# One v piece transposed by DMA ahead of the second weights, other first and last steps, in a fused attention and gated-product kernel

## The chip, the cores and the metric

The kernel runs on one core of a Trainium2 chip. The time is the device time of one execution in microseconds (us); most executions of one kernel agree within 0.3%. The granted clock is the share of TensorE's full rate that the profile's clock records give.

Engines are named as in the profile: PE is TensorE, DVE VectorE, ACT ScalarE, POOL GpSimd, SP SyncE. In the traces each of them keeps the order that the program gives: in experiment e3 below, ScalarE stands 3.7 us at one instruction of the norms, and the evictions behind it wait. GpSimd issues the loads that cast float32 to bfloat16. SyncE issues stores and DMA transposes.

## The reference

For each of four batches with 5824 tokens of 256 channels:

```python
qn = q / (norm(q, axis=tokens) + 1e-6);  kn = k / (norm(k, axis=tokens) + 1e-6)
s  = kn.T @ qn / tau                      # 256 x 256, tau = 1
a  = softmax(s, -1)                       # divided by (sum + 1e-9)
x  = v @ a                                # 5824 x 256
```

and over all 23296 tokens `((x @ w1) * (x @ w2)) @ w3 @ w_out`, with w1 and w2 of 256 x 1024, w3 of 1024 x 1024, w_out of 1024 x 256.

## The kernel before

The kernel folds the softmax matrix into w1 and w2 (`Wf`, one pair per batch) and w3 into w_out (`W_sb`, once). What remains for each chunk of 512 tokens and each of 8 column tiles j are two products `a` and `b` with transposed v (four 512-column matmuls), their elementwise product `ab`, and output products `o` (four 256-column matmuls).

Until `W_sb` exists the output products of batch 0 are deferred, and afterwards two steps' worth are made for each step. While batch n runs, q and k of batch n+1 are loaded in six pieces each and their product G (the scores) is slipped between the other matmuls.

GpSimd's queue carries the loads, and two kinds of waits that keep them apart:

```python
def gate():                                   # not before TensorE has got this far
    if last_ab[0] is not None:
        nc.gpsimd.tensor_copy(gate_t, last_ab[0][:1, :1])

def hold(src):                                # not before this transpose has landed
    nc.gpsimd.tensor_copy(gate_t, src)
...
        if b == 0:
            ...
            at(7.0, 0.5, lambda: transpose_half_on_pe(0, 1, 0, True))   # v piece 1 on TensorE
            at(8.0, 0.5, lambda: transpose_half_on_pe(0, 1, 1, False))
            at(15.0, 0.0, transpose_w3)                                 # DMA, SP
            at(15.0, 0.0, lambda: transpose_piece(0, 2))                # DMA, SP
            for jt in range(FT):
                at(26.0 + 1.2 * jt, 0.87, lambda jt=jt: w_unit(jt))     # w3 @ w_out
            moves = [("v", 0, 3, 29.0), ("qk", 1, 0, 38.0), ("qk", 1, 1, 43.0), ("v", 0, 4, 50.0), ("qk", 1, 2, 58.0)]
            moves += [("qk", 1, 3, 63.0), ("v", 0, 5, 70.0), ("qk", 1, 4, 81.0), ("qk", 1, 5, 87.0)]
            moves += [("v", 1, 0, 96.0), ("v", 1, 1, 106.0), ("v", 1, 2, 116.0), ("qk", 2, 0, 126.0)]
            t0, t1 = 57.0, 115.5              # the scores of batch 1 are spread over this stretch
...
        for nm, m, pi, t in moves:
            if before is not None:
                at(t, 0.0, lambda w=before: hold(...))   # the v piece moved before, transposed
            at(t, 0.0, gate)
            if nm == "qk":
                at(t, 0.0, lambda m=m, pi=pi: load_qk(m, pi))
                before = None
            else:
                at(t, 0.0, lambda m=m, pi=pi: load_piece("v", m, pi))
                at(t + 4.0, 0.0, lambda m=m, pi=pi: transpose_piece(m, pi))
                before = (m, pi)
```

The numbers after `at(` are a model clock of TensorE's work, which the emitter uses to sort instructions. They are no waits. So a load stands in GpSimd's queue in this order, and is issued when everything ahead of it in that queue is done. The all-reduce of the norms (`tot`, at t1 + 1) stands in the same queue.

"v 5" is the last v piece of batch 0, "q/k 1_4" the fifth q and k pieces of batch 1.

## Time and profile before

| | before |
|---|---|
| time, median of 6 | 573.16 us (572.88 to 575.41) |
| span of the profiled run | 571.7 us |
| PE busy | 559.4 us, 98% |
| last k piece of batch 0 landed | 31.5 us |
| first product with v | 40.69 us |
| w3 landed; its product starts | 59.8 us; 67.07 us |
| w3T and v 2 transposed (hold ends) | 72.96 us |

The timeline shows start, duration, engine and line, instruction, and in brackets the idle time before it and its releaser.

```profile
105.42 0.60 POOL L430 COPY gate_t<-vT 1x1 bf16<-1x1 bf16 x1 [12.71 <-DMA vT<-v]
...
111.29 1.04 POOL L426 COPY gate_t<-abs 1x1 bf16<-1x1 bf16 x1 [2.29 <-DVE abs L453]
112.27 0.53 POOL L106 DMA_DIRECT2D v<-in_v_dram  x1
...
127.40 0.18 POOL L430 COPY gate_t<-vTt 1x1 bf16<-1x1 bf16 x1 [14.05 <-DMA vTt<-v]
...
128.65 0.54 POOL L109 DMA_DIRECT2D k<-in_k_dram  x1
```

The hold of 105.42 ended late, but at 111.29 GpSimd waits for TensorE's progress (`gate_t<-abs`): the queue has caught up. Then v 5 is loaded, and k 1_4 cannot be issued before v 5 is transposed, at 127.4. TensorE meets k 1_4 at 139.19 without a wait. How small that slack is, the page does not say, but the trace does: the load issued at 128.65 landed at 138.89, 0.3 us ahead of its first use. k 1_5 landed at 143.72 and was first used at 148.74, so it had 5.0 us.

### The profile page before, as it was taken

The page shows a single profiled execution, that of the slowest core. Times are in us where ns is not written, and L with a number is a line of the kernel's source. Part 1 is how long each engine was busy: PE and PEld are TensorE (multiplying, and loading weights), DVE is VectorE, ACT ScalarE, POOL GpSimd, SP SyncE. Part 2 cuts the span into 40 slices and gives each one's busy share as a digit, 9 for nine tenths or more (in the row PEclk, how much of TensorE's full clock was granted, in tenths as well). Part 3 has the DMA queues.
Part 4 walks back from the last instruction along what each step waited for, and adds up shares of the span by engine and source line. Part 5 has one row for each costly group of instructions (what it writes and reads, how often), then busy time and mean ns, then how long its engine had stood idle before and what let it go on. Part 6 is the DMA issues. An engine that isn't in the chain of part 4 may idle for free.

```text
span 571.7 us, 10102 instructions
## 1 busy us (share of the span) xinstructions
PE 559.4 (98%) x3750; PEld 354.5 (62%) x3750; DVE 377.4 (66%) x612; ACT 337.7 (59%) x624; POOL 83.3 (15%) x164
## 2 busy tenths in 40 slices
PE   7789999999999999999999999999999999999997
PEld 4655576776666666666666666666665666666665
DVE  1047744788977567887776667778876656565564
ACT  0046644777856567776766567767766554454453
POOL 5250020303030111121030012031120000000000
PEclk9999999999999999999999999999999999999999
DMA  8999959869685697495661595665640325221011
GB/s 163 211 187 208 184 104 240 170 149 242 140 183 118 123 204 150 94 192 121 145 144 72 99 215 123 140 136 126 175 110 38 85 73 148 63 63 75 38 72 58
DMA packets 74560, 76.93 MB, mean 135 GB/s; under 512 B 54160, under 2 KB 58256, under 8 KB 74512
## 3 DMA queue, kind: packets, MB, share of 16 engines
q0 software_dynamic: 15504, 39.46, 39.3%
q1 hardware_dynamic: 58784, 36.64, 22.2%
q8 instruction: 29, 0.48, 0.3%
q10 hardware_dynamic: 224, 0.20, 0.1%
q14 instruction: 19, 0.16, 0.1%
HBM read 78.91 MB, written 23.86 MB: 180 GB/s over the span
## 4 chain that ended last, share of the span: by engine, by line
PE 92%; DMA 5%; DVE 1%; ACT 1%; POOL 1%; issue 0%; ACTq 0%; POOLq 0%
PE o L479 28%; PE a L438 27%; PE b L438 27%; PE G L188 5%; DMA k<-in_k_dram 5%; PE fold L349 2%; PE w L596 1%; ACT as L444 0%; ACT kr L279 0%; POOL k L109 0%; POOL q L109 0%; DVE abs L453 0%; PE sqk L221 0%; DVE vT L136 0%; DVE abs L455 0%
## 5 line engine op out<-in xcount | busy, mean ns | idle before, releaser
L453 DVE TENSOR_TENSOR abs<-as,b 128x512 bf16<-128x512 bf16 x336 | 230.5, 687 | 141.4 <-ACT as L444 130.3
L444 ACT CAST as<-a 128x512 bf16<-128x512 f32 (+1 forms) x384 | 216.1, 563 | 176.9 <-DVE abs L453 90.2
L438 PEld LDWEIGHTS <-Wf 128*128 128x128 bf16 x1536 | 149.2, 98 | 102.0 <-issue 1.9
L479 PE MATMUL o<-W_sb,abs 128*128 128x256 bf16 x1376 | 209.6, 273 | 0.1
L438 PE MATMUL a<-vT,Wf 128*128 128x512 bf16 x704 | 209.4, 379 | 0.2
L438 PE MATMUL b<-vT,Wf 128*128 128x512 bf16 x704 | 209.3, 379 | 0.0
L479 PEld LDWEIGHTS <-abs 128*128 128x128 bf16 x1376 | 134.5, 98 | 81.6 <-DVE abs L455 0.3
L197 DVE TENSOR_TENSOR acc<-acc,sq 128x1024 f32<-128x1024 f32 x66 | 80.4, 1219 | 0.4 <-ACT sq L185 0.3
L188 PE MATMUL G<-k,q 128*128 128x256 bf16 x276 | 49.9, 273 | 0.0
L185 ACT ACTIVATE sq<-q 128x512 f32<-128x512 bf16 x66 | 41.8, 634 | 0.0
L185 ACT ACTIVATE sq<-k 128x512 f32<-128x512 bf16 x66 | 41.6, 630 | 0.0
L426 POOL COPY gate_t<-abs 1x1 bf16<-1x1 bf16 x39 | 13.9, 355 | 167.7 <-DVE abs L453 167.0
L500 DVE COPY osb<-o 128x512 f32<-128x512 f32 x44 | 30.1, 685 | 0.7 <-PE o L479 0.7
L430 POOL COPY gate_t<-vT 1x1 bf16<-1x1 bf16 x17 | 4.4, 258 | 169.3 <-DMA vT<-v 134.0
L188 PEld LDWEIGHTS <-q 128*128 128x128 bf16 x276 | 27.0, 98 | 3.1
L499 ACT COPY osb<-o 128x512 f32<-128x512 f32 x44 | 25.8, 586 | 3.8 <-PE o L479 1.8
L279 ACT ACTIVATE kr<-row 128x256 f32<-128x256 f32 x1 | 0.4, 385 | 31.6 <-PE row L267 31.6
L109 POOL DMA_DIRECT2D q<-in_q_dram x29 | 15.7, 541 | 13.2 <-DMA k<-in_k_dram 6.0
L349 PE MATMUL fold<-w,e 128*128 128x512 bf16 x64 | 17.0, 380 | 0.5 <-DVE vT L136 0.4
L356 ACT ACTIVATE Wf<-fold,rs 128x512 bf16<-128x512 f32 x16 | 10.9, 688 | 8.1 <-PE fold L349 6.4
L244 DVE TENSOR_TENSOR dk<-sqk,ident 128x256 f32<-128x256 f32 x1 | 0.4, 425 | 21.3 <-PE sqk L221 21.3
L109 POOL DMA_DIRECT2D k<-in_k_dram x25 | 13.8, 551 | 3.7 <-DMA k<-in_k_dram 1.9
(89 smaller groups left out, 240.4 us busy)
## 6 DMA issues: line engine op xcount, KB each, us to landing
out_dram<-osb SPq DMA_DIRECT2D x44, 512.0 KB, 3.1
k<-in_k_dram POOLq DMA_DIRECT2D x19, 512.0 KB, 8.5
v<-in_v_dram POOLq DMA_DIRECT2D x19, 512.0 KB, 5.2
q<-in_q_dram POOLq DMA_DIRECT2D x18, 512.0 KB, 6.6
w_wout<-in_moe_w_dram POOLq DMA_DIRECT2D x1, 2048.0 KB, 23.6
k<-in_k_dram POOLq DMA_DIRECT2D x4, 320.0 KB, 9.9
v<-in_v_dram POOLq DMA_DIRECT2D x4, 320.0 KB, 5.4
q<-in_q_dram POOLq DMA_DIRECT2D x4, 256.0 KB, 12.0
```

The lines of the kernel that those rows point to most:

```text
L109: nc.gpsimd.dma_start(out=pieces[nm, n, pi][:, lo:hi, :], in_=qk_main[nm, n][0][:, pi * PIECE + lo : pi * PIECE + hi, :])
L185: nc.scalar.activation(out=dst[:, :, part, :], in_=src[:, o : o + 2, :], func=AF.Square)
L188: nc.tensor.matmul(G[:, ct, :], lhsT=qt[:, i, ct * P : (ct + 1) * P], rhs=kt[:, i, :], start=(pr == 0 and part == 0 and ct == 0), stop=(pr ...
L197: nc.vector.tensor_add(accs[n], accs[n], sqs[0])
L349: nc.tensor.matmul(st["fold", i], lhsT=st["e"][:, c2, c1 * P : (c1 + 1) * P], rhs=w12[:, c2, w, h * 512 : (h + 1) * 512], start=(c2 == 0), ...
L426: nc.gpsimd.tensor_copy(gate_t, last_ab[0][:1, :1])
L438: nc.tensor.matmul(t[:, :n], lhsT=Wf[b][:, ct, w, j * P : (j + 1) * P], rhs=rhs_of(b, c, ct), start=(ct == 0), stop=(ct == CT - 1),)
L444: nc.scalar.copy(a_sb[:, :n], tiles[0][:, :n])
L453: nc.vector.tensor_mul(ab, a_sb, tiles[1])
L479: nc.tensor.matmul(tl[h][:, o, :], lhsT=lhsT, rhs=W_sb[:, j, :], start=(j == 0 and o == 0), stop=(j == FT - 1 and (small or o == 1)), skip ...
L499: nc.scalar.copy(o[:, 0:2, :], tl[0])
L500: nc.vector.tensor_copy(o[:, 2:4, :], tl[1])
```

## The change

Its intent: start earlier, spend less TensorE time on transposes, and make the changes of batch smoother. The diff, cut to its core:

```diff
-    busy(14)
-    load_piece("k", 0, 0, (half,))
-    load_piece("q", 0, 0, (half,))
+    busy(10)
+    for nm in "kq":                            # first halves: plain loads by SP, cast on chip
+        new_piece(nm, 0, 0)
+        raw[nm] = work.tile([P, half, C], F32, tag="o_sb", ...)
+        nc.sync.dma_start(out=raw[nm], in_=qk_main[nm, 0][0][:, :half, :])
+        load_part(nm, 0, 0, half, PIECE)
...
+            nc.tensor.matmul(                  # sums start from 1e-9: a float32 matmul, per batch
+                st["sum"][:, :CT], lhsT=tiny, rhs=ones_pp[:1, :CT], start=True, stop=False, ...)
...
-            fold_mm(0, 0) ... fold(5, "out")   # six folds and a transpose before the first product
+            quarter_mm(0, c1, 0) ... quarter_mm(0, c1, 1)       # a quarter before, the rest after it
...
-            + [(0.2, 15.5, sums)]
-            + [(0.43, 16.5 + 0.85 * i, lambda i=i: fold(i)) for i in range(8)]
+            + [(0.2, 16.5, sums)]
+            + [(0.43, 17.5 + 1.1 * i, lambda i=i: fold(i)) for i in range(8)]
...
-    nc.gpsimd.dma_start(out=wout_sb, ...)      # right behind the load of v 2
-    nc.gpsimd.dma_start(out=w3_bf, in_=w3r)
...
-            at(7.0, 0.5, lambda: transpose_half_on_pe(0, 1, 0, True))
-            at(8.0, 0.5, lambda: transpose_half_on_pe(0, 1, 1, False))
-            at(15.0, 0.0, transpose_w3)
-            at(15.0, 0.0, lambda: transpose_piece(0, 2))
+            at(0.0, 0.0, lambda: transpose_piece(0, 2))
+            at(0.0, 0.0, lambda: transpose_piece(0, 1))
+            at(0.0, 0.0, lambda: hold(vTs[0][0][:1, PIECE, 0, :1]))
+            at(0.0, 0.0, load_w3)
+            at(16.0, 0.0, transpose_w3)
-                at(26.0 + 1.2 * jt, 0.87, lambda jt=jt: w_unit(jt))
+                at(35.0 + 1.2 * jt, 0.87, lambda jt=jt: w_unit(jt))
-            moves = [("v", 0, 3, 29.0), ("qk", 1, 0, 38.0), ...                                  t0, t1 = 57.0, 115.5
+            moves = [("qk", 1, 0, 29.0), ("v", 0, 3, 30.0), ("qk", 1, 1, 43.0), ("qk", 1, 2, 47.0), ("v", 0, 4, 53.0)]
+            moves += [("qk", 1, 3, 62.0), ("qk", 1, 4, 66.0), ("v", 0, 5, 72.0), ("qk", 1, 5, 81.0)]
+            moves += [("v", 1, 0, 94.0), ("v", 1, 1, 104.0), ("v", 1, 2, 114.0), ("qk", 2, 0, 126.0)]
+            t0, t1 = 54.0, 113.0
-            t0, t1 = 16.0, 104.0               # later batches
+            t0, t1 = 16.0, 98.0
```

At the end, outputs run five behind in the last chunk, the 64 left-over rows are multiplied first, and the last two outputs swap. The cut leaves out that w1 and w2 are loaded in three ranges of columns instead of two, and smaller moves.

## The prediction

> **What bounds the kernel now.** I read the page's busy shares first, then the busy time in stretches, then the chain of work, then the DMA landings.
>
> The page gives TensorE 559.4 us of 571.7. The stretches say where the other 12 us are:
>
> ```profile
> core 0: us, PE busy (x) PEld busy (x) DVE busy (x) ACT busy (x) POOL busy (x), PEclk, DMA share, GB/s
> 0.00:31.50 31.50, 25.44 (x264) 19.20 (x264) 1.94 (x11) 1.28 (x1) 12.43 (x26) 1.00 1.00 188
> 31.50:37.00 5.50, 4.24 (x42) 3.12 (x42) 2.16 (x9) 2.57 (x8) 5.23 (x8) 1.00 1.13 166
> 37.00:40.70 3.70, 3.33 (x25) 1.66 (x26) 2.01 (x5) 2.32 (x4) 0.49 (x2) 1.00 1.18 192
> 40.70:67.10 26.40, 26.40 (x142) 12.73 (x141) 21.06 (x32) 17.58 (x30) 0.00 (x0) 1.00 1.05 199
> ...
> 170.00:183.00 13.00, 12.86 (x94) 7.92 (x93) 9.59 (x31) 8.41 (x20) 1.45 (x4) 1.00 0.66 160
> ...
> 303.00:315.00 12.00, 11.88 (x94) 8.31 (x92) 8.82 (x25) 7.81 (x18) 0.00 (x0) 1.00 0.11 44
> ...
> 436.00:449.00 13.00, 12.59 (x92) 7.90 (x90) 9.31 (x27) 7.92 (x18) 0.00 (x0) 1.00 0.11 42
> ...
> 561.80:572.00 10.20, 5.91 (x58) 4.92 (x56) 4.96 (x19) 3.41 (x10) 0.00 (x0) 0.95 0.22 77
> ```
>
> The reader sees that from 40.7 us on TensorE is full except at the three changes of batch and at the end; before 31.5 us the DMA share is 1.00. So there are two limits in series: the load of the first q and k, then TensorE's issue rate. Busy time flatters, since a matmul's record is longer than its turn: in the order of starts a 512-column matmul follows the last after 216 ns, a 256-column one after 109. Counting what starts exceed that by, the empty time is 0.90 us at 170 to 183, 0.58 at 303 to 315, 1.48 at 436 to 449, 0.54 after 560.
>
> The chain of work names the start:
>
> ```profile
> 4.52 11.89 DMA k<-in_k_dram
> 16.69 14.79 DMA k<-in_k_dram
> 31.53 0.84 PE sqk L221 x12
> ...
> 37.70 0.89 PE fold L349 x4
> 38.59 0.46 PE tr_I-511_512 L132 x8
> 39.05 0.02 issue
> 39.07 0.70 DVE vT L136
> 39.77 0.04 issue
> 39.82 1.04 PE fold L349 x4
> ```
>
> The last k piece lands at 31.5, the softmax of the first batch takes until 37.0, and then 3.7 us go by until the first product with v, with a stop at the evacuation of a transposed half of v.
>
> The weights' chain, from the DMA view and the timeline, matters for the rival:
>
> ```profile
> w_wout<-in_moe_w_dram POOLq DMA_DIRECT2D x1, 2048.0 KB, 23.6
> vT<-v SPq DMA_TRANSPOSE x22, 3.7
> w3T<-w_wout SPq DMA_TRANSPOSE x4, 4.4
> 67.07 1.04 PE L596 MATMUL w<-w_wout,w3T 128*128 128x256 bf16 x8
> ```
>
> w3, issued at 36.19, lands at 59.8; its transposes start at 59.85, and its product starts at 67.07, 3 us after the first transpose can have landed.
>
> **What the Trainium skill says.** "DMA: Bandwidth & Descriptors", section SWDGE vs HWDGE vs iDMA: a load that casts must come from GpSimd; loads issued by SP are plain, are fed to the same 16 engines on other queues, and each engine takes turns between them. So the new plain loads of the first halves add no bandwidth. The section "Latency and other measured facts" has a shorter time to the first byte for SP's path (about 0.6 against 1 us). The trace agrees in sign: an output issued by SP near 564.4 moves its first packet at 565.23 (some 0.85 us), the first load of GpSimd, issued at 1.22, at 2.60 (1.4 us). "TensorE: Matmul & The Clock Gate", The HAM clock gate, says that a fresh TensorE runs at half rate for about 3.4 us. The trace agrees: warm-up matmuls are 427 ns apart at first and 216 later. Taking four away at the start is harmless only while TensorE waits for loads anyway, which it does.
>
> **The change, part by part.**
>
> *First loads.* SP can issue at about 0.75 us (its start wait ends at 0.7), so data flow from about 1.65 instead of 2.60: 0.95 us. In addition the first 105 packets of before took 251 ns each, against 173 later, and moved only half the full rate until 4.5 us, a loss of about 0.85 us, part of which a second queue can fill. A plain 4096-byte packet takes 163 ns (outputs), a casting one with the same 4096 bytes read takes 173, so the plain loads are not dearer. The queue is then full until 28 us, so an earlier start carries through to 31.5. I book 1.2 us. The two casts (VectorE, ScalarE) lie where both engines idle. The last pieces are issued in the same eight-deep order, so they shift alike.
>
> *First folds.* Before, from 37.0 to the first product at 40.69: six folds and a transpose; afterwards two more folds (0.86 us) and three transposes (1.35). Changed: sums and a first quarter of 8 matmuls of 256 columns (0.87 us), one small operation less on the sums, evacuation of 256 columns (the kr activation of that size took 0.39, the scaling of s 0.42), so first product at about 38.6; afterwards the second quarter (0.87), four folds (1.73) and one transpose (0.45). TensorE time to the same point: 40.69 + 2.21 = 42.9 against 38.6 + 3.05 = 41.7. The two removed transposes (0.9 us) and the one moved into the wait for the exponentials (0.45) are in this; the second v piece is now transposed by the DMA. Gain 1.2, less 0.1 for a possible wait at the third product, whose factors VectorE delivers just then: 1.1 us.
>
> *Changes of batch.* The built order shows the sums earlier in all three, and in the last two the folds in pairs between 512-column products of chunk 10, where before three came at once; in the first they stand singly from chunk 11's start. A pair costs VectorE 0.69 + 0.75 us and ScalarE 0.56 + 0.69 in a step of 2.16 us on TensorE, and four PSUM buffers turn over once in a step, so these should not stop. At the chunk of 192 columns VectorE and ScalarE still have the outputs of chunk 10 to copy (0.69 and 0.59). I estimate 1.2 us of the 2.96 left: gain 1.75. Against it three extra float32 matmuls that start the sums: the float32 one already there (turned) has two passes 155 ns apart, so about 0.25 us each, 0.75 in all. Net gain 1.0 us.
>
> *End.* With a lag of five, ten output matmuls (1.1 us) cover the last evacuation, worth the 0.5 us that is empty now; but the first products of the last chunk come 0.33 us apart without outputs, while VectorE needs 0.4 to 0.5 each (0.29 + 0.21, partly overlapped), and the order of the two outputs moves the ACT-issued store 0.1 us later. I book zero.
>
> *Moved only.* w3's product has the same matmuls, later. Deferred outputs reach 43 pieces; before they were some 34. There is room for 54 (16 held in the q buffers, 38 in the pool).
>
> Sum: 1.2 + 1.1 + 1.0 = 3.3 us gained.
>
> **The rivals.**
>
> *The weights come too late.* w_out and w3 now wait for the transposes of v pieces 2 and 1. Before, piece 2 landed near 46.4; the smaller w1 and w2 loads (512-byte packets, 60 ns each, against 98 for 1024) cost about 0.5 us more, the earlier start gives 1.2 back: 45.7. Two transposes, 5.6 us: 51.3. Then 0.4 gate, 1.8 to the first packet, 3.4 for w_out, 10.2 for w3, 0.75 to land (their times of before): 67.9. First transpose of w3 usable 3.7 to 4.4 later: 71.6 to 72.3. The product's place in the order: 37.4 (38.6 less the load gain) + 37 products at 0.864 + 3.05 = 72.4. So the slack is zero to 0.8 us: a wait of 1 to 2 us is quite possible, and then TensorE stops, since nothing is ordered around it. I book 0.4 us as its mean. Further down, v piece 3 is usable at about 93 for a need near 94.6.
>
> *The first loads hide nothing*, if the slow first packets belong to the engines and not to the queue, or if the last small pieces of q are paced by their issue: then the load part is 0.5 or less, and the time about 570.9.
>
> *The batch changes don't improve*, because the float32 matmuls wait or the small chunk stays short of VectorE: then that part is minus 0.7, and the time 571.8.
>
> All three failing together with a 2 us wait would give no gain at all. None of these can come to 2% (11.5 us).
>
> **Range and chances.** 572.96 - 3.3 + 0.4 = 570.06, taken as 570.1. The best case (load 1.8, no wait, batch changes 1.7, end 0.4) gives 568; the poor ones 572. Range 568.4 to 572.1. Faster by over 2%: 0.01; within 2%: 0.97; slower: 0.02, for a starved stretch in batch 0 that I have not seen.
>
> **What would show it.** The last k piece should land near 30.3 and the first product with v start near 37.4. The first w matmul should start near 72.4 with no wait on w3T before it; a gap there makes the rival true. The empty time at the batch changes should fall from 2.96 to about 1.2 us without the new float32 matmuls. At the end, the gap before the last outputs should be gone and a few small ones appear at chunk 11. The prediction is wrong if the first products start no earlier than 38.5, or if TensorE stops for over 2 us between 72 and 130 us.

## More of the kernel before

The prediction reads the page. One row of it that the prediction leaves out matters later. It is from the costliest groups; the last columns are the engine's idle time just before the group, and what ended most of it:

```profile
L430 POOL COPY gate_t<-vT 1x1 bf16<-1x1 bf16 x17 | 4.4, 258 | 169.3 <-DMA vT<-v 134.0
```

GpSimd stands 169 us in the holds of this group. That alone costs nothing.

## The result, and the profile after

| | before | after |
|---|---|---|
| time, median (6 runs each) | 573.16 us | 577.52 us (576.87 to 578.74) |
| ratio of the fast runs | | 1.0075, 95% interval 1.0056 to 1.0094 |
| span of the profiled run | 571.7 us | 576.7 us |
| last k piece of batch 0 landed | 31.48 | 30.22 |
| first product with v | 40.69 | 37.63 |
| w3 product | 67.07, no wait | 72.88, after a wait of 0.17 |
| hold on w3T (after), v 2 (before) ends | 72.96 | 78.86 |
| time less span, profiled run | 1.7 | 2.0 |

A ratio is the mean time of one kernel's fast runs over that of the other's of the same rounds, so it is not quite the ratio of the medians. Executions over 1.5% slower than the fastest of the same kernel are left out of the means. The changed kernel is slower by 0.75%, and not faster by 0.5% as predicted. Its profiled execution is the slowest of its six, 1.2 us above the median: what follows accounts for 5.0 us of span, of which the medians show 4.4.

The busy time in stretches, as in the prediction's first view (after each engine's busy time its instructions; then the granted clock, the DMA share and GB/s):

```profile
core 0: us, PE busy (x) PEld busy (x) DVE busy (x) ACT busy (x) POOL busy (x), PEclk, DMA share, GB/s
0.00:30.30 30.30, 25.70 (x261) 19.58 (x262) 2.67 (x13) 2.33 (x2) 11.50 (x24) 1.00 1.01 211
...
72.00:140.00 68.00, 67.99 (x492) 47.71 (x490) 48.23 (x64) 44.25 (x82) 14.41 (x33) 1.00 0.83 183
140.00:152.00 12.00, 8.90 (x53) 5.67 (x52) 6.20 (x8) 5.41 (x10) 0.00 (x0) 0.86 0.81 179
152.00:187.00 35.00, 34.04 (x237) 21.94 (x236) 22.07 (x49) 19.59 (x43) 7.29 (x11) 1.00 0.68 167
```

Of the kernel before, the same two last stretches:

```profile
140.00:152.00 12.00, 12.00 (x83) 7.83 (x81) 10.53 (x14) 9.76 (x19) 1.23 (x3) 1.00 0.74 172
152.00:187.00 35.00, 34.86 (x230) 21.22 (x228) 25.58 (x58) 22.80 (x48) 6.24 (x10) 1.00 0.67 140
```

The start did what was predicted. The largest loss sits in 140 to 152: 53 recorded matmuls instead of 83, and a granted clock of 0.86. The timeline of TensorE there:

```profile
142.98 0.60 PE L513 MATMUL o<-W_sb,abs 128*128 128x256 bf16 x4
146.68 0.38 PE L191 MATMUL G<-k,q 128*128 128x256 bf16 x2 [3.10 <-DMA k<-in_k_dram]
146.90 0.78 PE L472 MATMUL a<-vT,Wf 128*128 128x512 bf16 x2
147.47 1.06 PE L472 MATMUL b<-vT,Wf 128*128 128x512 bf16 x2
```

TensorE stops for the load of k 1_5. The stop is 3.10 us in the profile's measure and 3.27 us counted from start to start. Afterwards a pair of 512-column matmuls takes 0.78 to 1.06 us instead of 0.59: until 151 us they come at half rate, which loses another 1.4 us (4.66 us of empty time between 140 and 150, less 3.27).

Why k 1_5 is late, the chain of work that ended last says (start, duration, what; the chain followed back from the end):

```profile
75.03 3.71 DMA w3T<-w_wout
...
80.80 9.77 DMA v<-in_v_dram
90.59 3.69 DMA vT<-v
...
98.32 12.50 DMA v<-in_v_dram
110.84 3.72 DMA vT<-v
...
118.95 12.24 DMA v<-in_v_dram
...
164.86 3.20 POOL tot L261
```

In the kernel before this chain consists, over nearly the whole of batch 0, of TensorE's matmuls. Now it is load, transpose, load, transpose, and finally the all-reduce. The holds are those that GpSimd had before, but two, on v 1 and on w3T, stand in place of the first one on v 2:

```profile
L464 POOL COPY gate_t<-vT 1x1 bf16<-1x1 bf16 x17 | 4.7, 275 | 164.5 <-DMA vT<-v 164.5
L464 POOL COPY gate_t<-w3T 1x1 bf16<-1x1 bf16 x1 | 0.2, 177 | 24.0 <-DMA w3T<-w_wout 24.0
```

With the holds on the last pieces of v (33.2 us, before 31.2) GpSimd now stands 221.7 us in holds, against 200.5. A sum over the execution does not show the cause (c2 below, the fastest kernel here, has 205.2); the position does. The chain begins at 78.86 instead of 72.96, v 5 is issued at 118.4 instead of 112.3, and the queue does not catch up with TensorE before q/k 1_5. That load had 5.0 us of slack. Now it lands at 146.64, which is 2.9 us later, and TensorE asks for it at 143.4, which is 5.3 us earlier: 5.0 less 2.9 less 5.3 is -3.2, the stop. (k 1_4, which the new order loads ahead of v 5, lands 4.8 us before its use; k 1_1 and k 1_3 land only 0.3 and 0.04 us before theirs.)

For a ledger I used a view that neither busy time nor gaps give: ScalarE evicts each of the 384 `a` products once, and all 384 are recorded, so the start of the k-th eviction in one trace less that in before's is the lead (negative) or lag. Inside batch 0 this is distorted where deferred outputs stand elsewhere; at chunk 2 and from batch 1 on it is exact. The columns hold the profiled runs of the experiments told below; before's own profiled run took 573.43 us, 0.3 above its median:

| at | before, us | after | h1 | b1 | b3 | c2 | g1 | g2 |
|---|---|---|---|---|---|---|---|---|
| batch 0, chunk 2 | 57.3 | -2.14 | -1.74 | -1.52 | -0.10 | -1.58 | -2.55 | -2.28 |
| batch 1 | 182.8 | 4.87 | 0.87 | -1.01 | 1.55 | -1.58 | -0.41 | -0.24 |
| batch 2 | 315.6 | 4.96 | 0.86 | -1.01 | 1.19 | -1.94 | -0.18 | -0.56 |
| batch 3 | 448.8 | 4.50 | 0.86 | -1.29 | 0.31 | -2.82 | -0.63 | -1.44 |
| end of span | 571.7 | 5.01 | 0.78 | -1.45 | 0.26 | -2.97 | -0.10 | -0.94 |

The changed kernel is 2.14 us ahead at chunk 2 and 4.87 behind at batch 1: 7.0 us are lost in batch 0 and at its end, and next to nothing after that.

### The profile page after: what moved, and what is told of

It reads as the page before. It is cut to its first block, busy times and chain, and to the rows that moved or that the text cites. A ratio compares the mean times of both kernels' runs of the same rounds, so it can differ in the third digit from the quotient of the medians.

```text
span 576.7 us, 10110 instructions
## 1 busy us (share of the span) xinstructions
PE 562.3 (98%) x3745; PEld 355.4 (62%) x3745; DVE 377.6 (65%) x609; ACT 338.9 (59%) x626; POOL 79.3 (14%) x165
## 4 chain that ended last, share of the span: by engine, by line
PE 75%; DMA 17%; POOL 3%; ACT 2%; issue 2%; DVE 1%; SPq 0%; POOLq 0%; ACTq 0%
PE a L472 24%; PE b L472 23%; PE o L513 21%; DMA v<-in_v_dram 9%; PE G L191 3%; DMA k<-in_k_dram 3%; DMA vT<-v 3%; PE fold L359 2%; DMA q<-in_q_dram 2%; POOL k L112 1%; POOL q L112 1%; ACT as L478 1%; DMA w3T<-w_wout 1%; POOL gate_t L460 1%; POOL tot L261 1%
## 5 line engine op out<-in xcount | busy, mean ns | idle before, releaser
L460 POOL COPY gate_t<-abs 1x1 bf16<-1x1 bf16 x39 | 10.1, 260 | 167.2 <-DVE abs L487 166.4
L359 PE MATMUL fold<-w,e 128*128 128x512 bf16 x56 | 15.2, 379 | 0.0
L112 POOL DMA_DIRECT2D v<-in_v_dram x25 | 13.4, 540 | 4.1 <-issue 3.2
```

The costliest lines, as they stand in the source:

```text
L112: nc.gpsimd.dma_start(out=pieces[nm, n, pi][:, lo:hi, :], in_=qk_main[nm, n][0][:, pi * PIECE + lo : pi * PIECE + hi, :])
L359: nc.tensor.matmul(m, lhsT=st["e"][:, c2, c1 * P : (c1 + 1) * P], rhs=w12[:, c2, w, lo:hi], start=(c2 == 0), stop=(c2 == CT - 1),)
```

## The experiments

My theory was that GpSimd's chain of loads and holds runs some 6 to 10 us behind what it was, and TensorE meets its links. The rivals were that one badly placed load is to blame, that DMA bandwidth is, or that the loss comes from the small parts (float32 matmuls, folds).

### First group: one suspect each, on the changed kernel

**e1: q/k 1_5 ahead of v 5.**

```diff
-... ("v", 0, 5, 72.0), ("qk", 1, 5, 81.0)]
+... ("qk", 1, 5, 72.0), ("v", 0, 5, 81.0)]
```

> The changed kernel with one swap: the last q and k pieces of batch 1 are loaded before v piece 5 of batch 0, not after it. Theory (queue of holds: GpSimd issues those loads only when the transposes of v piece 5 have ended, at 135.0 us): they are issued near 118 us, land near 131, the 3.1 us stop of TensorE at 143 goes, so do its slow matmuls after it (1.4 us) and most of the 1.7 us extra empty time at the first change of batch; about 571.3 us, 6 us under the changed kernel. Rival (bytes: the DMA engines simply have too much to move between 80 and 146 us): v piece 5 then comes late instead, TensorE stops at chunk 10 near 165 us, and the time stays within 2 us of 577.5.

Measured: 577.88 us (577.53 to 581.62), ratio 1.0085. The stop at 143 is gone, and TensorE stops 2.64 us at 124 for k 1_3, which stands behind the same chain, and 1.4 and 0.7 us at 167 to 170. In the changed kernel k 1_3 landed at 123.82 for a use at 123.86; here, with more loads issued right behind it, it landed at 126.76. The expected gain did not come; the time is the rival's, the place of the stop is not.

**e2: w3 loaded early, right behind v 2, without the wait for v 1's transpose.**

```diff
-            at(0.0, 0.0, lambda: hold(vTs[0][0][:1, PIECE, 0, :1]))
-            at(0.0, 0.0, load_w3)
+    (both loads behind load_piece("v", 0, 2), as in the kernel before)
```

> The changed kernel, but w_out and w3 are loaded right behind v piece 2 as before, without waiting for the transposes of v piece 1, which stay on the DMA. Theory (the wait of the weights starts the chain of holds 8 us late): w3 lands near 60, its transposes end near 71, the last q and k of batch 1 land near 138, the stop at 143 goes; about 571.3 us. Rival (the order protects the transposes): the transposes of v piece 1, sharing the engines with the w3 load, end after 55 us, TensorE stops at chunk 2, and more than 2 us of the gain is lost again there.

Measured: 584.89 us, ratio 1.0201, the worst of all. From TensorE's timeline:

```profile
65.32 1.03 PE L472 MATMUL a<-vT,Wf 128*128 128x512 bf16 x2 [10.87 <-DMA vT<-v]
```

The transposes of v 2 and v 1 were issued from 48 us on and landed at 63.5 and 65.3, after w3's load had landed at 62.1. From 50 to 58 us they moved 0.13 MB beside 1.47 MB of loads; in the changed kernel, with no load beside them, they moved 1.02 MB from 48 to 52 us. So these transposes came almost to a stand behind the queued loads. After the stop TensorE ran at half rate until 70.5 us. The hold that the change put in is needed once v 1 is transposed by DMA. This is the rival side of that test, and it won.

**e3: the scores of batch 0 end 2.5 units later.**

```diff
-            t0, t1 = 54.0, 113.0
+            t0, t1 = 54.0, 115.5
```

> The changed kernel with the scores of batch 1 spread until 115.5 on the order's clock, as before, in place of 113; loads untouched. Theory (late data for an in-order TensorE): the last products of scores are asked for some 2.2 us later, so the stop shrinks from 3.1 to about 1 us and the slow matmuls after it (1.4 us) do not appear[...]; 577.5 - 3.6 = about 574. Rival (the stop is not tied to when the scores are asked for, only the whole chain of loads counts): 577 or more.

Measured: 577.42 us (575.87 to 579.58), ratio 1.0064. The stop for k 1_5 is gone; in its place TensorE stops 3.1 us at 166 for an eviction by ScalarE, which itself waits in order behind the norms: `tot` starts at 165.3, after the hold on v 1_1. Half-rate matmuls follow this stop too (granted clock 0.50 from 170.7 to 174.1). At 72 us TensorE also waits 1.5 us for w3T. It is a different link of the same queue: the rival's time came, but for another reason.

**e4 and e4b: the titled part undone, all else kept.** The same kernel was run twice.

```diff
+    (w_out and w3 loaded right behind load_piece("v", 0, 2))
-            at(0.0, 0.0, lambda: transpose_piece(0, 2)); transpose_piece(0, 1); hold(...); load_w3
+            at(7.0, 0.5, lambda: transpose_half_on_pe(0, 1, 0, True))
+            at(8.0, 0.5, lambda: transpose_half_on_pe(0, 1, 1, False))
+            at(15.0, 0.0, transpose_w3); at(15.0, 0.0, lambda: transpose_piece(0, 2))
     (product at 26.0 + 1.2 * jt, moves, t0 and t1 of batch 0 as in the kernel before)
```

> The changed kernel with its second part undone: v piece 1 is transposed on TensorE, w_out and w3 are loaded behind v piece 2, their product and all loads of batch 0 stand where they stood before; first loads, quarters, sums, later batches and end stay changed. Theory (only the reordering of batch 0 costs): the stop at 143 goes; the gains of the start stay less the 0.9 us of the transposes; about 571.3 us, 1.8 under the kernel before. Rival (other parts of the change cost too, the sums or the end): 573 or more.

> The same kernel as e4 (the changed kernel with the batch-0 work on v piece 1 and on w3 put back as before), run again because its profile fell in an execution at half clock. Theory (GpSimd's queue of holds, loads and all-reduce is late against TensorE): the time repeats at 578 to 581, and the trace shows TensorE stopped once or twice in batch 0 or just after its end, 3 to 8 us in all, each time for a DMA landing or for the all-reduce behind GpSimd's holds. Rival (the cost lies in the parts that stayed, such as the small float32 matmuls or the folds of the later batches): no stop over 1 us before 170 us, and the extra time spread over the changes of batch.

Measured: 579.51 us over the five fast executions, ratio 1.0104, and again 576.84 us, ratio 1.0066. (The record's 579.93 for the first counts the slow execution in.) The first run's profile fell in that execution of 1197.52 us, with TensorE at half rate throughout, and says nothing on this question. Why the two medians lie 2.7 us apart isn't settled; the fast executions of e4 list a granted clock of 0.993 to 0.996, those of e4b 0.997 to 1.000, so the first had more half-rate time. The profile of e4b is of its fastest run (575.27 us): a stop of 1.6 us at 135 us for q/k 1_4, then 2.2 us of empty time at the change of batch against 0.9 before.

What follows: undoing that part alone does not restore the time, so my first picture, in which it carried the whole loss, is too small. The kernel before's own order of batch 0 also stops when TensorE comes earlier.

### Second group: single parts of the change on the kernel before

**b1: the plain first loads alone.**

```diff
-    busy(14); load_piece("k", 0, 0, (half,)); load_piece("q", 0, 0, (half,))
+    busy(10); raw[nm] = ...; nc.sync.dma_start(out=raw[nm], ...); load_part(nm, 0, 0, half, PIECE)
+    nc.vector.tensor_copy(pieces["k", 0, 0][:, :half, :], raw["k"])
+    nc.scalar.copy(pieces["q", 0, 0][:, :half, :], raw["q"])
```

> The kernel before with the new first loads alone (first halves of k and q 0 as plain loads from SP, cast by VectorE and ScalarE, ten warm-up matmuls). If an earlier start carries through: last k piece lands 1.2 us earlier and the time falls by 1.0 to 1.3 us (571.7 to 572.0). Rival (TensorE arriving earlier uses up the slack of the loads of batch 0): the last k piece lands earlier, but a stop of 1 us or more appears between 67 and 170 us and the time is the same or up to 3 us longer.

Measured: 572.24 us, ratio 0.9986 (0.9972 to 0.9999). The lead at chunk 2 is 1.52 us. From it 0.25 us lie outside the span (time less span is 2.0 instead of 1.75 us), and 0.5 us go at 138 us, where TensorE now waits for q/k 1_4. This load landed at 138.15, 0.74 us earlier than before; with the 0.3 us of slack that it had, that covers 1.0 of the 1.52 us, and the rest is the stop. Both theories are partly right.

**b3: the new spacing of scores, sums and folds alone**, without the float32 matmuls.

```diff
-            + [(0.2, 15.5, sums)] + [(0.43, 16.5 + 0.85 * i, ...)]
+            + [(0.2, 16.5, sums)] + [(0.43, 17.5 + 1.1 * i, ...)]
-            t0, t1 = 57.0, 115.5    # batch 0        t0, t1 = 16.0, 104.0   # later
+            t0, t1 = 57.0, 113.0    # batch 0        t0, t1 = 16.0, 98.0    # later
```

> The kernel before with only the spacing of scores, sums and folds of the changed kernel (scores end at 113 in batch 0 and 98 later, sums and folds spread wider), without the float32 matmuls that start the sums. My prediction's term: empty time at the three changes of batch falls from 2.96 to about 1.2 us, time 571.2 (570.7 to 571.8). Rival (scores that end earlier meet the last q and k of the batch before they have landed, or the folds still stop TensorE): time 573 to 576, with a wait on k before a G matmul.

Measured: 573.74 us, ratio 1.0012. The scores that end earlier in batch 0 meet the same load: 1.4 us at 136. In the later batches the lag falls from 1.55 to 0.31 us, which is a gain of 1.24 us. One part of the spacing pays, and the other takes it back.

**b4: the end alone.**

```diff
+                lag = LAG_END if b == B - 1 and c == NCH - 1 else LAG      # LAG_END = 5
-        for s, lhsT in enumerate(lhs):
+        for s, lhsT in reversed(list(enumerate(lhs))) if small else enumerate(lhs):
     (and the product of the left rows ahead of the other in the last chunk)
```

> The kernel before with only the end changed (outputs five behind in the last chunk, left rows first, outputs reversed). Prediction's term: zero, time within 0.4 us of before. Rival: 0.5 us gained if the last gap is covered, or 0.5 us lost if the products of the last chunk wait for VectorE.

Measured: 573.18 us against 573.07, ratio 1.0000. Zero, as predicted.

**h1: the titled part alone.**

```diff
-    (w_out and w3 right behind v 2; v 1 on TensorE; product at 26.0 + 1.2 * jt)
+            at(0.0, 0.0, lambda: transpose_piece(0, 2))
+            at(0.0, 0.0, lambda: transpose_piece(0, 1))
+            at(0.0, 0.0, lambda: hold(vTs[0][0][:1, PIECE, 0, :1]))
+            at(0.0, 0.0, load_w3)
     (w3's transposes, product and moves of batch 0 as in the changed kernel)
-            t0, t1 = 57.0, 115.5
+            t0, t1 = 54.0, 115.5
```

> The kernel before with only the part that the title of the change names: v piece 1 transposed by DMA ahead of the loads of w3 and w_out, their product later, and the order of batch 0's loads that goes with it (scores of batch 0 end at 115.5 as before). Nothing of the start, the sums, the folds or the end. Theory (this part starts GpSimd's chain of loads and holds about 6 us later, TensorE arrives 0.9 us earlier for the two transposes it no longer makes, so batch 0 stops): w3T's hold ends near 79 instead of 73, one stop of 1 to 3 us between 120 and 172 us or a late all-reduce, time 573.5 to 576. Rival (by itself the part is free and only the earlier start or the earlier scores turn it into stops): no stop over 1 us, time 571.8 to 573.2.

Measured: 574.84 us (574.19 to 576.77), ratio 1.0035 (1.0020 to 1.0049). The part is no gain by itself. Its hold on w3T ends at 79.25 instead of 72.96. TensorE is 1.74 us ahead at chunk 2 and 0.87 behind at batch 1: 2.6 us lost. No single stop exceeds 1 us in its profile (0.4 on v 3 at 93, 0.9 at 167), and the change of batch, with `tot` at 164.0, has 2.3 us of empty time. The time was expected, the stop smaller than expected. The traces split this loss. The 0.9 us at 167 follow from ScalarE's wait of 1.6 us for `tot`. The 2.3 us after 170 do not: c1 below has the same 2.3 us, though ScalarE does not wait for `tot` there. What h1 and c1 share is that ScalarE waits for VectorE's scaled scores ahead of both exponentials, as it does not in the kernel before (the first of the two in h1, c1 and before):

```profile
172.89 0.51 ACT L318 ACTIVATE e<-s,r 128x256 bf16<-128x256 f32 x1 [1.09 <-DVE s L313]
173.72 0.51 ACT L318 ACTIVATE e<-s,r 128x256 bf16<-128x256 f32 x1 [1.09 <-DVE s L313]
171.97 0.51 ACT L318 ACTIVATE e<-s,r 128x256 bf16<-128x256 f32 x1
```

So where the softmax stands in the order matters beside the queue. The part contains the new order of loads; the two transposes alone were not run.

### Third group: links of the chain on the changed kernel

**f2: no hold for v 4.**

```diff
-            if before is not None:
+            if before is not None and before != (0, 4):
```

> The changed kernel without one hold: in batch 0 GpSimd issues q/k 1_3 and 1_4 without waiting for the transpose of v piece 4 (that piece is needed only near 130 us). Theory (the chain of load, transpose, hold on GpSimd runs some 10 us behind and TensorE meets its last links): q/k 1_3 is issued near 101 us instead of 116, q/k 1_5 at 126 to 133 instead of 136, the 3.27 us stop before a G matmul at 143 us shrinks below 0.7 us or goes, and no half-rate stretch follows; the transpose of v4 ends later (124 to 130 instead of 114.7). Time 575 or less, unless the all-reduce still comes late. Rival (DMA bandwidth, not the holds, is the limit of batch 0): k 1_5 lands no earlier than 145 and the stop stays, or v4's transpose starves and TensorE stops over 2 us at its first product, time 577 or more.

Measured: 576.97 us, ratio 1.0068; the profiled run is the fastest (575.01 us). q/k 1_3 is issued at 102.6, q/k 1_5 at 131 to 133, and the stop for k is gone. k 1_5 lands at 138.84 instead of 146.64, so the bytes alone had not kept it late; but with the loads let go, the DMA engines are 90% busy or more from 97 to 128 us. A new one appears. SyncE's timeline, then the same transpose in the changed kernel, the chain of work, and TensorE's timeline:

```profile
110.17 9.39 SPq L158 DMA_TRANSPOSE vT<-v  x1
110.84 1.65 SPq L158 DMA_TRANSPOSE vT<-v  x1
119.66 8.12 DMA out_dram<-osb
128.50 0.38 PE L513 MATMUL o<-W_sb,abs 128*128 128x256 bf16 x2 [2.98 <-ACT osb L533]
```

With more loads in flight SyncE stands 9.39 us at v 4's transpose instead of 1.65, so the store behind it is issued 7 us later than in the changed kernel (119.66 for 112.59), and takes 8.1 us itself. That duration is not new: stores of batch 0 in the kernel before take 2.9 to 9.0 us (median of the execution 3.1). The buffers of outputs run out, ScalarE waits for one, and TensorE for ScalarE. The holds protect the stores, through SyncE's queue, as well as the transposes. I had not thought of the stores. The time lies between theory and rival; the theory's 575 or less was missed.

**f4: the all-reduce ahead of the wait for v 1_1.**

```diff
-... ("v", 1, 2, 114.0), ("qk", 2, 0, 126.0)]
+... ("v", 1, 2, 115.0), ("qk", 2, 0, 126.0)]
```

> The changed kernel with v piece 1_2 of batch 0 moved one clock unit later, so that GpSimd runs the all-reduce of the norms before it waits for v 1_1. Theory (the all-reduce late in GpSimd's queue holds up ScalarE, whose evictions then stop TensorE at the first change of batch): tot starts before 160 us instead of 164.86, the empty time at 160 to 187 falls from about 2.3 us to 1.3 or less, the stop at 143 stays; time 576 to 576.8. Rival (that loss comes from the small float32 matmuls and the folds): empty time there within 0.3 us of before the edit, time 577 to 578.

Measured: 577.17 us, ratio 1.0064. `tot` starts at 159.8, and ScalarE no longer waits for it. Empty time from 160 to 187 falls from 2.33 to 1.45 us, not quite to the 1.3 expected. The stop for k 1_5 stays (3.1 us), with half-rate matmuls after it for longer than in the changed kernel, so the median gains only 0.35 us. The mechanism is right; the time expected was missed by 0.4 us.

**f5: both edits**, the lines of f2 and f4 together.

> Both edits, no hold after v4 and the all-reduce first, in the changed kernel. Theory: the losses before 187 us fall from 7.0 us (lead of 2.14 at the second chunk to lag of 4.87 at batch 1) to 1.5 to 3, time 571.5 to 573.5. Rival: the loss moves to another stop, as in the runs with the pieces swapped and with the scores later, time 576 to 578.

Measured: 575.99 us (575.69 to 576.90), ratio 1.0053. The stores stop TensorE for 3.1 us at 126, as in f2, and w3T for 0.9 us. The rival is right: the loss moved.

**g1: scores later and the all-reduce ahead of the wait.**

```diff
-            t0, t1 = 54.0, 113.0
+            t0, t1 = 54.0, 115.5
-... ("v", 1, 2, 114.0), ("qk", 2, 0, 126.0)]
+... ("v", 1, 2, 117.5), ("qk", 2, 0, 126.5)]
```

> The changed kernel with batch 0's scores ending at 115.5 and v 1_2 issued after the all-reduce. Theory (the stop at 143 is k 1_5 behind the holds, the stop at 166 that replaced it when only the scores were later is the all-reduce behind the hold on v 1_1): both go, leaving a wait on w3T of 0.2 to 1.5 us and 1.5 us at the change of batch; time 573 to 574.5. Rival (the loss moves on to a further link): another stop over 2 us, 576 to 578.

Measured: 573.26 us (572.72 to 574.22), ratio 0.9999. Three numbers in the emitter give back 4.3 us. No stop exceeds 0.74 us between chunk 1 and batch 1, and in the two stretches in question the clock is granted in full:

```profile
140.00:152.00 12.00, 12.00 (x90) 8.65 (x89) 10.20 (x13) 8.94 (x17) 0.00 (x0) 1.00 0.86 204
152.00:187.00 35.00, 33.99 (x230) 21.52 (x229) 23.24 (x52) 19.93 (x43) 7.62 (x13) 1.00 0.73 163
```

This settles where the larger part of the loss was: later scores alone (e3) met the all-reduce, the earlier all-reduce alone (f4) met k 1_5, and both together meet neither. A part remains: of the 2.55 us of lead at chunk 2, 2.1 are gone by batch 1. 0.7 us go to w3T, and the first change of batch still has 2.3 us of empty time, although `tot` starts at 156.1 and nothing waits for it.

**g2: g1 without the float32 matmuls.**

```diff
-            nc.tensor.matmul(st["sum"][:, :CT], lhsT=tiny, rhs=ones_pp[:1, :CT], start=True, stop=False, ...)
-                    start=False, stop=...
+                    start=(c1 == 0 and c2 == 0), stop=...
-                nc.vector.reciprocal(rs, m[:, :CT])
+                nc.vector.tensor_scalar_add(rs, m[:, :CT], 1e-9); nc.vector.reciprocal(rs, rs)
```

> As g1, with the sums as before (no float32 matmul that starts them, 1e-9 added by VectorE). Theory: the three float32 matmuls in the later batches and the one in the first cost 0.25 to 0.4 us each, so 0.8 to 1.3 us less than g1. Rival: their time was idle anyway, within 0.4 us of g1.

Measured: 571.96 us (571.54 to 572.76), 1.30 us less than g1. In g1's trace 0.63 us pass from the last output matmul ahead of the sums to the first product after them, in g2's 0.21 us: 0.41 us for each of the three later batches, 1.2 in all.

### Fourth group: towards a version that beats both

**c1: the kernel before with the plain loads and the spacing of the later batches**, scores of batch 0 one unit later.

```diff
     (the lines of b1)
+            + [(0.2, 15.5 if n == 1 else 16.5, sums)]
+            + [(0.43, 16.5 + 0.85 * i if n == 1 else 17.5 + 1.1 * i, lambda i=i: fold(i)) ...]
-            t0, t1 = 57.0, 115.5    # batch 0        t0, t1 = 16.0, 104.0   # later
+            t0, t1 = 57.0, 116.5    # batch 0        t0, t1 = 16.0, 98.0    # later
```

> The kernel before with the parts that paid: the plain first loads, and in the later batches the scores that end at 98 with the wider sums and folds; batch 0 as before with its scores ending one unit later. Expected: 0.8 (as measured with the loads alone) to 1.3 (with the 0.5 us wait on k gone) plus 1.2 (the lag of the batch-change run against before falls by 1.24 us from batch 1 to batch 3) makes 570.5 to 571.1, faster than both kernels. Rival: the wait on k 1_5 grows or the later scores push the all-reduce into the change of batch, and the sum is 571.5 to 573.

Measured: 572.98 us (572.05 to 574.03), ratio 0.9996: nothing gained. TensorE waits 1.9 us for q/k 1_4 at 138 in the profiled run, the slowest of five, and the first change of batch has 2.3 us of empty time, without a wait for `tot`. The rival holds.

**c2: as c1, but q/k 1_4 ahead of v 5** in batch 0, and its scores as in the kernel before.

```diff
-... ("qk", 1, 3, 63.0), ("v", 0, 5, 70.0), ("qk", 1, 4, 81.0), ("qk", 1, 5, 87.0)]
+... ("qk", 1, 3, 63.0), ("qk", 1, 4, 67.0), ("v", 0, 5, 73.0), ("qk", 1, 5, 83.0)]
```

> The kernel before with the plain first loads, the later batches' scores, sums and folds of the changed kernel, and in batch 0 q/k 1_4 issued ahead of v 5 (batch 0's scores end at 115.5 as before). Theory (the start's gain is lost because q/k 1_4, which waits for v5's transposes, lands just after TensorE needs it, near 138): no stop over 0.5 us before 170 us, the lead of 1.5 us at chunk 2 is kept to batch 1, the later batches add 1.2, less 0.25 us that lie outside the span: 570.2 to 570.9. Rival (some other load of batch 0 takes its place): a stop of 1 to 2 us elsewhere in batch 0 and 571.5 to 573.

Measured: 570.82 us (570.71 to 571.13), ratio 0.9955 (0.9933 to 0.9978). It is faster than both kernels. In the ledger the lead of 1.58 us is kept whole to batch 1, and the later changes of batch add 1.24. Two things differ from c1, the order and one unit of the scores: the wait of 1.9 us is gone, and the first change of batch has 1.2 us of empty time. GpSimd's timeline shows k 1_4 issued ahead of v 5, and v 5 still early enough (2.5 us later than before), since its gate still waits for TensorE:

```profile
109.25 0.54 POOL L109 DMA_DIRECT2D k<-in_k_dram  x1
113.84 1.04 POOL L426 COPY gate_t<-abs 1x1 bf16<-1x1 bf16 x1 [4.05 <-DVE abs L453]
114.82 0.52 POOL L106 DMA_DIRECT2D v<-in_v_dram  x1
```

**c3: c2 with the all-reduce first.**

```diff
-... ("v", 1, 2, 116.0), ("qk", 2, 0, 126.0)]
+... ("v", 1, 2, 117.5), ("qk", 2, 0, 126.5)]
```

> As c2, with v 1_2 of batch 0 issued after the all-reduce. Theory: tot starts near 158 instead of 161, the empty time at 170 to 187 (0.9 to 1.1 us) falls by 0.3 to 0.7 us: 569.6 to 570.5. Rival: the change of batch was not waiting for tot here; within 0.2 us of c2.

Measured: 570.96 us, the same as c2. Here the change of batch was not waiting for `tot`. The rival holds.

## Why the prediction was wrong

The time on record was 570.1 us, the range ended at 572.1, and 577.5 came. (The sum started from 572.96 us for the kernel before; the median is 573.16, which changes nothing.) Step by step:

**First loads, booked -1.2: right.** The last k piece lands 1.26 us earlier. The first packet moves at 1.77 us (1.65 expected, 2.60 before); the first 105 packets of the new queue are hardly faster, 238 ns each against 251, as the rival feared. Alone the part gave 0.83 us of time, for the two reasons told at b1.

**First folds, booked -1.1: half.** Leads at chunk 2 are 2.14 us for the changed kernel and 1.52 for the loads alone, so 0.6 us remain for the folds and the two transposes off TensorE. The first product itself came as predicted (37.63 for 37.4); more of the work came back after it than I counted. In e4b, which has the new folds but the transposes on TensorE again, the lead is 1.16 us, less than with the loads alone, so the gain here comes from the transposes and not from the folds.

**Changes of batch, booked -1.75: right for two of three.** The last two gain 1.24 us (b3). The first became 1.7 us worse (2.6 against 0.9 us of empty time from 150 to 187). 0.9 us of that are the all-reduce behind the holds (f4). The rest is not, since g1 has 2.3 us there with the all-reduce early; ScalarE's waits for the scaled scores, told at h1, are there in the changed kernel as well.

**Float32 matmuls, booked +0.75: mis-sized.** They measure 1.2 to 1.3 us. I counted two passes of 155 ns each. The trace has 93 ns of empty time ahead of them, then 132 and 178 ns.

**End, booked 0: right** (b4).

**w3's product, booked +0.4: right, partly by luck.** It waits 0.17 us in the changed kernel, but 0.3 to 1.5 in e1, e3, f4, f5, g1 and g2. Its chain was read some 1 us too early: v 2 had landed at 47.2 us before, not at 46.4, and w3 landed at 69.0 instead of 67.9.

**The step that failed** is the rival of late weights and its sentence "Further down, v piece 3 is usable at about 93 for a need near 94.6". v 3 was indeed in time. But I followed the chain to its first two links only, and took the rest of batch 0 as unchanged. From 72.96 to 78.86 the start of everything behind w3T moves by 5.9 us. TensorE comes 2.1 us earlier, and the scores are placed 2.5 units earlier still. At k 1_5 this became a landing 2.9 us later and a use 5.3 us earlier, for which the kernel before had 5.0 us of slack; TensorE stopped for 3.27 us. "A starved stretch in batch 0 that I have not seen" had a chance of 0.02 in my text; "if TensorE stops for over 2 us between 72 and 130 us" named the right sign with a window that ended too early, for the stop came at 143.

The ledger of the 7.0 us between chunk 2 and batch 1: 3.27 for k 1_5, 1.4 of half-rate matmuls, 0.17 for w3T, 1.7 at the first change of batch, 0.4 for the float32 matmul there. The sum is about 6.9.

On the half rate: the Trainium skill, "TensorE: Matmul & The Clock Gate", HAM oscillation, states the rule "no PE-idle gaps >~3.4µs", and section The HAM clock gate says that the activity window runs freely, so the outcome varies. The traces agree with the second more than with the first. In the profile's measure of idle time, stops of 3.10 us (after), 2.95 (f4) and 2.92 (e3) were each followed by half-rate matmuls; one of 2.98 (f2) and one of 2.94 (f5) were not, nor was one of 2.48 (e1). Stops of about 3 us were thus a lottery for 1.4 us or more, which may widen the spread of the kernels with such stops (576.9 to 578.7 for the changed kernel, 575.9 to 579.6 for e3; 570.7 to 571.1 for c2). That it makes up the spread was not shown: the kernel before, without a stop in its profile, ranges from 572.6 to 577.5 over all rounds.

**What is shown and what stays open.** Shown: the titled part costs 0.35% by itself (h1); a TensorE that comes earlier, or scores that stand earlier, stops at q/k 1_4 in the kernel before (b1, b3); the stop for k 1_5 with its half-rate stretch, and the all-reduce that a later order meets in its place, make up the larger part of the loss (g1 gives back 4.3 us); the float32 matmuls cost 1.3 us (g2). Argued only: that the waits ahead of the exponentials make the 2.3 us at the first change of batch in h1, c1 and g1; no run moved the softmax alone. Open: the 2.7 us between two runs of the same kernel (e4 and e4b).

## What to carry to other kernels

When one queue carries loads, waits for transposes and a reduction, follow it link by link until it next waits for the compute engine, and give each link its slack in the kernel before. A change that moves the queue later and the compute earlier spends that slack twice. If removing one stop leaves the time alone, look for the next link of the same queue before looking for another cause. Here a better order of the loads (c2) paid, and taking two transposes off TensorE (h1) did not.

## What the Trainium skill lacked or had wrong

- "DMA: Bandwidth & Descriptors", Rules for kernel authors, says "A transpose next to ordinary DMAs needs nothing". That speaks of correctness; of time the page has nothing there. In e2 the transposes moved 0.13 MB in 8 us beside the queued loads of w3 and w_out, against 1.02 MB in 4 us alone in the changed kernel, and TensorE stopped for 10.87 us.
- The same page has nothing on how long a store takes behind queued loads: up to 9.0 us in batch 0 of the kernel before and 8.8 in f2, where the median over the execution before is 3.1.
- "TensorE: Matmul & The Clock Gate", HAM oscillation: idle gaps of 2.92, 2.95 and 3.10 us, under the 3.4 us of its rule, were followed by matmuls at half rate, and gaps of 2.94 and 2.98 us were not. The page's closing table, Why this matters for your kernels, has about 3 us instead, which does not sort these gaps either.
- The same page, Seeing it yourself, warns of unreliable clock records and of a clock gate seen stuck for over 50 us. Here one execution of e4 ran at half rate to the end: 443 ns from one 512-column matmul to the next instead of 216, and 1197.52 us instead of 580, while its clock records gave 1.00.
- No page that I found gives the cost of a tiny float32 matmul among bfloat16 ones: 0.4 us each in g1 (0.63 us against 0.21 in g2), with 93 ns of empty time ahead of the first pass, then 132 and 178 ns.
